# Where the powers of lam for waves 2 to 5 are computed, and which engine makes one of four turn copies

## The chip, the cores and the metric

The kernel runs on one core of a Trainium2 chip. The core has a matrix engine (TensorE, in the profile PE, with its weight loads as PEld), three engines for elementwise work (VectorE or DVE, ScalarE or ACT, GpSimd or POOL), and SyncE (SP), which here only issues transfers between the chip's main memory and the on-chip memory. ACT and POOL can issue transfers too. Each engine runs its own instructions in their order; engines wait for one another through semaphores. Matmul results land in a small accumulator memory (PSUM), everything else that is on the chip is in SBUF. The metric is device time in microseconds, as the median of several runs.

## The reference

Two stages. The first is a linear attention with a decay per head, over 4 batches, 8 heads, 768 positions and head size 64, worked in blocks of 64 positions:

```python
rel = pos[:, None] - pos[None, :]
Dmask = np.where(rel >= 0, lam[:, None, None] ** rel[None, :, :], 0.0)
lam_pow = lam[:, None, None] ** (pos[None, :, None] + 1)
for b in range(nb):
    intra = np.einsum('bhic,bhjc->bhij', qb, kb) * Dmask[None]
    intra = np.einsum('bhij,bhjd->bhid', intra, vb)
    inter = np.einsum('bhid,bhde->bhie', qb * lam_pow[None], kv_state)
    out[:, :, sl] = intra + inter
    kb_dec = kb * rev_pow[None]
    kv_state = lam_block[None, :, None, None] * kv_state + np.einsum('bhsd,bhse->bhde', kb_dec, vb)
```

`lam` has one value for each head, between 0.97 and 0.99. The second stage is an MLP on the 3072 rows of 512 that come out: `h = x @ w_in` (512 to 2048), `g = h * sigmoid(1.702 h)`, `g @ w_out` (2048 to 512).

## The kernel before

The work is cut into six waves of 512 rows. Wave 0 takes the first 256 positions of batches 0 and 1, wave 1 those of batches 2 and 3, and waves 2 to 5 take 128 further positions of all four batches each. In a wave the attention of its positions is computed in transposed form (`xT`), and the MLP runs on that. The list `main` (line 543 on) holds the MLP's matmul groups of all waves in order; the list `side` holds the attention of the next wave with a position in `main` at which each part is issued. So each engine's order is fixed when the kernel is built, and PE is meant to find MLP matmuls between the attention's short ones.

The kernel applies the decay by scaling k and q with powers of lam before the scores are taken. Waves 0 and 1 (`ND = 2`) use `kd_pow` and `qd_pow`; their casts are line 198. Waves 2 to 5 use four other tables:

- `k_pow` and `q_pow` (128 x 2 x 8: position x copy x head): lam to the power 127 - s and s + 1. Read by the casts of line 205.
- `inv_pow` (128 x 8): lam to the power -128. Read with the 0/1 mask by line 335.
- `blk_pow` (128 x 4): lam to the power 128 for the heads of each half. Read by the state update, line 355.

All tables are made at the start. `lam` (8 values) is loaded by a transfer on ACT's queue, spread over 128 partitions by a matmul with ones (`lam_p`, line 147), ACT takes the logarithm (`ln_lam`, line 149), and then each table is one or two ACT instructions, exp(scale * ln_lam), with the exponents of each position in small tables made by POOL's iota (`i_k`, `i_q`, lines 127 to 130). In the order of the code: kd_pow and qd_pow (line 152), then, as the first lines of the hand-written schedule, k_pow and q_pow (455), inv_pow (456), blk_pow (458). Line 460 is a GELU on one column, which makes ACT load the table set of the GELU before it is needed.

After that comes the hand-written start of wave 0. A "turn" is a transposition on PE into PSUM (`turn_pe`, line 228; its PE instructions are line 234) and a copy from there to SBUF by the engine that is passed as `copy` (ACT's copies bear line 217, DVE's line 214). For batch 0 k is cast and turned in two groups, and then q in two groups; all four copies are ACT's. `fill` issues matmuls on zeros, whose result nobody reads. `d_scores` makes scores on PE (255) and masks on DVE (259); `d_one`, `d_state`, `d_inter` and `d_out` make the block's state and output on PE (271, 290, 308). Batch 1 of the wave follows, its k cast by POOL, its q by DVE, with the copies of the second groups by DVE.

Transfers: SP issues the loads of k, q and v of wave 0 at once, batch 0 first. POOL waits for v's first element (`gate_pool`, line 447) and issues the loads of w_in (line 177) and, after batch 1's v cast, the rest of w_in and w_out (181). The last POOL instruction of this stretch is the affine_select that makes `mask` (502). SP's loads of wave 1 stand behind a small transfer that reads w_out's second part (`gate_sync`, line 450). POOL is used again for wave 1's v cast (line 211) and for one of its k casts.

Of the kernel before, what the change touches and what calls it, by code (L numbers as in the profile page):

```python
# [24 lines left out]
def kernel(  # L25
# [13 lines left out]
    nc = tc.nc  # L39
    f32 = mybir.dt.float32  # L40
    bf16 = mybir.dt.bfloat16
    B, H, S, D = q.shape
    P = 128
# [10 lines left out]
    EXP = mybir.ActivationFunctionType.Exp  # L54
    LN = mybir.ActivationFunctionType.Ln
    COPY = mybir.ActivationFunctionType.Copy
    GELU = mybir.ActivationFunctionType.Gelu_apprx_sigmoid
    MUL = mybir.AluOpType.mult
    ADD = mybir.AluOpType.add

    NW = S // P

    const = ctx.enter_context(tc.tile_pool(name="const", bufs=1))
# [4 lines left out]
    op = ctx.enter_context(tc.tile_pool(name="op", bufs=4))  # L68
# [39 lines left out]
    def iota(x, pattern, base, cm):  # L108
        nc.gpsimd.iota(x, pattern=pattern, base=base, channel_multiplier=cm, allow_small_or_imprecise_dtypes=True)

    A, Z = slice(0, 64), slice(64, P)
# [15 lines left out]
    i_k = const.tile([P, 1], f32)  # L127
    iota(i_k, [[0, 1]], P - 1, -1)
    i_q = const.tile([P, 1], f32)
    iota(i_q, [[0, 1]], 1, 1)  # L130
    mask = const.tile([P, 1, P], bf16)
    nc.gpsimd.memset(mask, 1.0)

# [2 lines left out]
    def acc(name, dt=f32, shape=None, tag="a"):  # L136
        return ps.tile(shape or [P, 4, P], dt, tag=tag, bufs={"a": 5, "mm": 3}[tag], name=name)

    def fill(n, new=None):
        if new:  # L140
            fill_ps[0] = acc("ps_fill", shape=[P, W], tag=new)
        for _ in range(n):
            nc.tensor.matmul(fill_ps[0], zero[:, 0:P], zero, start=True, stop=True)  # L143

    fill(4, "mm")
    lam_p = ps.tile([P, H], f32, tag="a", bufs=5, name="lam_p")
    nc.tensor.matmul(lam_p, ones, lam_r, start=True, stop=True)
    ln_lam = const.tile([P, H], f32)
    nc.scalar.activation(ln_lam, lam_p, LN)

    def mk_pow(x, scale):
        nc.scalar.activation(x, ln_lam, EXP, scale=scale)

    kd_pow = const.tile([P, H, 2], f32)
    qd_pow = const.tile([P, H, 2], f32)
# [3 lines left out]
    k_pow = const.tile([P, 2, H], f32)  # L159
    q_pow = const.tile([P, 2, H], f32)  # L160
    inv_pow = const.tile([P, H], f32)
    blk_pow = const.tile([P, NP], f32)
    warm = const.tile([P, 1], f32)
# [16 lines left out]
    def load_w_out(j):  # L180
        nc.gpsimd.dma_start(
            out=w_out_sb[j], in_=moe_w_out.rearrange("(fc fi) d -> fi fc d", fi=P)[:, j * CW : (j + 1) * CW, :])
# [6 lines left out]
    def do_cast(w, c, nm, eng, g=None):  # L189
        if g in (None, 0):  # L190
            cast[w, c, nm] = work.tile([P, 2, HD], bf16, tag=f"{nm}s{c}", name=f"{nm}s")
        f, x = loaded[w, c, nm], cast[w, c, nm]
        if w < ND:
            pw = {"k": kd_pow, "q": qd_pow}[nm]
            for R in (0, 1) if g is None else (g,):
                for j in range(2):
                    h = slice(4 * R + 2 * j, 4 * R + 2 * j + 2)
                    eng.tensor_tensor(x.rearrange("p a (r i j d) -> p r j i a d", i=2, j=2, d=D)[:, R, j],  # L198
                                      f[:, h].rearrange("p i (a d) -> p i a d", a=2),
                                      pw[:, h].unsqueeze(3).to_broadcast([P, 2, 2, D]), op=MUL)  # L200
        else:
            pw = {"k": k_pow, "q": q_pow}[nm]
            n = 2 * H // 4
            for j in range(2):
                eng.tensor_tensor(x.rearrange("p b (r i j d) -> p j (b r) i d", i=2, j=2, d=D)[:, j],  # L205
                                  f.rearrange("p h (a d) -> p (h a) d", a=2).rearrange("p (n j i) d -> p j n i d", j=2, i=2)[:, j],
                                  pw.rearrange("p b (r j i) -> p j (b r) i", i=2, j=2)[:, j].unsqueeze(3).to_broadcast([P, n, 2, D]),
                                  op=MUL)
# [19 lines left out]
    def turn_pe(w, c, nm, copy=act_copy, g=None):  # L228
        x = cast[w, c, nm]
        rr = list(range(NP)) if g is None else [2 * g, 2 * g + 1]  # L230
        t = acc("ps_t", bf16, [P, len(rr), 2, P])
        for i, r in enumerate(rr):
            for a in range(2):
                nc.tensor.transpose(t[:, i, a, :], x[:, a, r * P : (r + 1) * P], ident)  # L234
        if g in (None, 0):
            trans[w, c, nm] = work.tile([P, 2 * NP, P], bf16, tag=f"{nm}T{c}", name=f"{nm}T")
        copy(trans[w, c, nm][:, 2 * rr[0] : 2 * rr[0] + 2 * len(rr)], t.rearrange("p r a s -> p (r a) s"))
# [106 lines left out]
    def n_state(w, R):  # L344
# [8 lines left out]
        for i in range(2):  # L353
            p = 2 * R + i
            nc.vector.scalar_tensor_tensor(new[:, :, p, :], old[:, :, p, :], blk_pow[:, p : p + 1], ps_kv[:, i],  # L355
                                           op0=MUL, op1=ADD)

# [93 lines left out]
        nc.sync.dma_start(out=behind, in_=x)  # L451

    with tc.manual_schedule():
        for x, i in ((k_pow, i_k), (q_pow, i_q)):
            nc.scalar.activation(x, ln_lam.unsqueeze(1).to_broadcast([P, 2, H]), EXP, scale=i)
        mk_pow(inv_pow, -1.0 * P)
        for j, rows in enumerate((A, Z)):
            nc.scalar.activation(blk_pow[rows].rearrange("p (r i) -> p r i", i=2),
                                 ln_lam[rows].rearrange("p (r j i) -> p r j i", i=2, j=2)[:, :, j, :], EXP, scale=1.0 * P)
        nc.scalar.activation(warm, q_pow[:, 0, 0:1], GELU)  # L460
        fill(5)
        for g in range(2):
            do_cast(0, 0, "k", nc.vector, g)
# [1 line left out]
            fill(2)  # L465
        for g in range(2):
            do_cast(0, 0, "q", nc.vector, g)
            turn_pe(0, 0, "q", act_copy, g)
            fill(2 - 2 * g)
        gate_pool(loaded[0, 0, "v"][0:1, 0, 0:1])  # L470
        load_w_in(0)
# [27 lines left out]
            load_w_in(j)  # L499
        for j in range(NCH):  # L500
            load_w_out(j)
        nc.gpsimd.affine_select(mask, mask, pattern=[[0, 1], [1, P]], channel_multiplier=-1, base=0,
                                compare_op=mybir.AluOpType.is_ge, fill=0.0)
        gate_sync(w_out_sb[1][0:1, 0, 0:2])
# [15 lines left out]
        def end(w, c):  # L520
# [11 lines left out]
            if w:  # L532
                nc.vector.tensor_tensor(kv_sb[0][:, 2 * w + c], kept[w, c], t, op=ADD)
            else:
# [9 lines left out]
        for w in range(NW):  # L544
# [3 lines left out]
            x = w + 1  # L548
# [57 lines left out]
```

## Time and profile before

| | |
|---|---|
| median of 8 runs | 208.19 us (207.49 to 209.06) |
| the profiled execution's own time | 208.26 us |
| its span | 206.6 us |
| PE busy | 198.6 us (96%) |
| DVE, ACT, POOL busy | 89.2, 86.0, 16.1 us |
| ACT's activations for k_pow, q_pow, inv_pow, blk_pow | 4.89 to 5.78 us from the span's start |
| table load of line 460 | from 5.80 us, 1.28 us long |
| first MLP matmul group of the stretch that then runs without a gap | 18.45 us |
| casts of wave 1's k on DVE | from 38.04 us |
| first use of k_pow, inv_pow, blk_pow | 53.4, 66.0, 76.6 us |

Line numbers are those of the kernel before. In lines of a timeline the first number is the start in us from the span's start, the second the length in us; then come engine, line, operation, what is written and read, how many instructions are taken together, and in brackets how long the engine sat idle before them and what ended that. In the chain of what ended last, listed in order of time, the two numbers are start and length as well. An engine name with a q behind it (SPq, POOLq) is its issuing side. A line of a helper is used by many parts of the kernel, so tile names say more than lines.

### The profile page before, as it was taken

What the parts mean: (1) busy time and instruction counts of PE and PEld (TensorE: products, weight loads), DVE (VectorE), ACT (ScalarE), POOL (GpSimd) and SP (SyncE); (2) the same over time, 40 slices, a digit from 0 to 9 for tenths busy, and PEclk for the clock granted to TensorE, in tenths of its full rate; (3) what the DMA queues carried; (4) which work ended last, traced back from release to release, by engine and by line L of the source; (5) the groups of instructions that cost most, each with busy time, mean ns of one, the idle gap of its engine ahead of it and who ended that gap; (6) DMA issues with size and microseconds to landing.
All of it is one profiled execution on the core that took longest, in us unless ns stands there. A gap on an engine that the chain in (4) does not pass through costs nothing.

```text
span 206.6 us, 4269 instructions
## 1 busy us (share of the span) xinstructions
PE 198.6 (96%) x1806; PEld 104.9 (51%) x1830; DVE 89.2 (43%) x158; ACT 86.0 (42%) x158; POOL 16.1 (8%) x37
## 2 busy tenths in 40 slices
PE   7989999999999999999999999999999999999994
PEld 2567444467864464444464444464444454444453
DVE  1685000686952842931743931743841731100121
ACT  4956662157665030565030566021566021565000
POOL 4369000060000000000000000000000000000000
PEclk9999999999999999999999999999999999999999
DMA  5999999999997999879961389971360111100112
GB/s 155 317 234 179 182 204 236 316 321 232 242 220 185 224 245 261 193 180 253 234 195 51 107 183 257 220 205 52 102 155 0 40 64 51 51 0 0 54 51 102
DMA packets 87640, 33.82 MB, mean 164 GB/s; under 512 B 67398, under 2 KB 84678, under 8 KB 87622
## 3 DMA queue, kind: packets, MB, share of 16 engines
q1 hardware_dynamic: 82868, 29.37, 56.3%
q0 software_dynamic: 4752, 4.19, 13.2%
q8 instruction: 14, 0.23, 0.4%
q14 instruction: 4, 0.03, 0.1%
q10 hardware_dynamic: 2, 0.00, 0.0%
HBM read 27.26 MB, written 6.29 MB: 162 GB/s over the span
## 4 chain that ended last, share of the span: by engine, by line
PE 90%; DVE 4%; ACT 3%; issue 1%; ACTq 0%; DVEq 0%
PE ps_out L413 39%; PE ps_h L389 35%; PE ps_h L401 5%; DVE sm L259 2%; PE ps_s L327 2%; PE ps_o L377 2%; PE ps_t L234 1%; PE ps_o L364 1%; DVE o_sb L417 1%; PE ps_s L255 1%; PE ps_fill L143 1%; PE ps_o L308 1%; PE ps_kv L351 1%; ACT L460 1%; PE ps_kv L271 1%
## 5 line engine op out<-in xcount | busy, mean ns | idle before, releaser
L413 PE MATMUL ps_out<-w_out,g_sb 128*128 128x512 bf16 (+2 forms) x400 | 83.8, 362 | 1.1 <-issue 0.6
L389 PE MATMUL ps_h<-xT,w_in 128*128 128x512 bf16 x330 | 73.2, 379 | 0.3
L391 ACT ACTIVATE g_sb<-ps_h 128x512 bf16<-128x512 f32 x84 | 50.2, 597 | 45.1 <-PE ps_h L389 45.1
L413 PEld LDWEIGHTS <-g_sb 128*128 128x128 bf16 x416 | 38.2, 98 | 41.0
L389 PEld LDWEIGHTS <-w_in 128*128 128x128 bf16 x336 | 32.9, 98 | 39.2
L417 DVE COPY o_sb<-ps_out 128x512 f32<-128x512 f32 (+2 forms) x26 | 16.9, 650 | 52.4 <-PE ps_out L413 52.3
L335 DVE SCALAR_TENSOR_TENSOR sm<-ps_s,inv_pow,mask 128x512 bf16<-128x512 f32 x32 | 21.8, 743 | 28.5 <-PE ps_s L327 22.3
L381 ACT CAST xT<-ps_o 128x512 bf16<-128x512 f32 x16 | 8.2, 599 | 37.8 <-PE ps_o L377 37.8
L198 DVE TENSOR_TENSOR ks<-kf,kd_pow 128x256 bf16<-128x256 f32 x8 | 2.9, 421 | 22.0 <-DMA kf<-in_k_dram 18.7
L401 PE MATMUL ps_h<-xT,w_in 128*128 128x256 bf16 x96 | 11.4, 273 | 0.0
L259 DVE TENSOR_TENSOR sm<-ps_s,mask_d 128x512 bf16<-128x512 f32 x16 | 9.9, 683 | 1.9 <-PE ps_s L255 1.8
L205 DVE TENSOR_TENSOR qs<-qf,q_pow 128x512 bf16<-128x512 f32 x16 | 10.3, 684 | 0.0
L205 DVE TENSOR_TENSOR ks<-kf,k_pow 128x512 bf16<-128x512 f32 x16 | 10.3, 683 | 0.0
L401 PEld LDWEIGHTS <-w_in 128*128 128x128 bf16 x96 | 9.0, 98 | 1.7 <-DVE xT L214 0.2
L403 ACT ACTIVATE g_sb<-ps_h 128x512 bf16<-128x512 f32 x12 | 7.2, 597 | 4.4 <-PE ps_h L401 4.3
L143 PE MATMUL ps_fill<-zero 128*128 128x512 bf16 x18 | 6.9, 510 | 1.4 <-DVE zero L113 1.4
L355 DVE SCALAR_TENSOR_TENSOR kv<-kv,blk_pow,ps_kv 128x256 bf16<-128x256 bf16 x12 | 5.0, 477 | 6.0 <-PE ps_kv L351 6.0
L217 ACT COPY kT<-ps_t 128x512 bf16<-128x512 bf16 (+1 forms) x5 | 3.7, 752 | 7.7 <-PE ps_t L234 7.7
L198 DVE TENSOR_TENSOR qs<-qf,qd_pow 128x256 bf16<-128x256 f32 x16 | 6.0, 428 | 1.1 <-DMA qf<-in_q_dram 1.0
L327 PEld LDWEIGHTS <-kT 64*128 64x128 bf16 x128 | 3.6, 94 | 3.4 <-issue 3.4
L214 DVE CAST v_sb<-vf 128x1024 bf16<-128x1024 f32 x8 | 5.1, 685 | 0.0
L327 PE MATMUL ps_s<-qT,kT 64*128 64x128 bf16 x128 | 5.0, 217 | 0.0
(66 smaller groups left out, 88.7 us busy)
## 6 DMA issues: line engine op xcount, KB each, us to landing
vf<-in_v_dram SPq DMA_DIRECT2D x11, 512.0 KB, 6.5
kf<-in_k_dram SPq DMA_DIRECT2D x10, 512.0 KB, 5.7
qf<-in_q_dram SPq DMA_DIRECT2D x10, 512.0 KB, 6.4
out_dram<-o_sb SPq DMA_DIRECT2D x15, 256.0 KB, 2.0
out_dram<-o_sb SPq DMA_DIRECT2D x17, 128.0 KB, 2.4
w_out<-in_moe_w_out_dram POOLq DMA_DIRECT2D x4, 512.0 KB, 13.8
w_in<-in_moe_w_in_dram POOLq DMA_DIRECT2D x3, 512.0 KB, 6.8
kf<-in_k_dram SPq DMA_DIRECT2D x4, 256.0 KB, 3.1
```

Source lines behind the costliest of these rows:

```text
L143: nc.tensor.matmul(fill_ps[0], zero[:, 0:P], zero, start=True, stop=True)
L198: eng.tensor_tensor(x.rearrange("p a (r i j d) -> p r j i a d", i=2, j=2, d=D)[:, R, j], f[:, h].rearrange("p i (a d) -> p i a d", a=2), p ...
L205: eng.tensor_tensor(x.rearrange("p b (r i j d) -> p j (b r) i d", i=2, j=2, d=D)[:, j], f.rearrange("p h (a d) -> p (h a) d", a=2).rearran ...
L259: nc.vector.tensor_tensor(sm.rearrange("p i a s -> p i (a s)"), s2[h].rearrange("p (i a) s -> p i (a s)", i=2), mask_d.rearrange("p o a b ...
L327: nc.tensor.matmul(s2[h][:, b, :], kT[hs, (b % 2) * NP + p, :], qT[hs, (b % 2) * NP + p, :], start=True, stop=True)
L335: nc.vector.scalar_tensor_tensor(sm, s, inv_pow[:, n : n + 1], mask.to_broadcast([P, B, P]), op0=MUL, op1=MUL)
L381: nc.scalar.copy(xT[w][:, p, :], ps_o.rearrange("p b s -> p (b s)"))
L389: nc.tensor.matmul(h, w_in_sb[j][:, kc, i * P : (i + 1) * P], xT[w][:, kc, :], start=(kc == 0), stop=(kc == KC - 1))
L391: nc.scalar.activation(g_of[w][:, fc, :], h, GELU)
L401: nc.tensor.matmul(h[:, u, :], w_in_sb[j][:, kc, i * P : (i + 1) * P], xT[w][:, kc, cols], start=(kc == 0), stop=(kc == KC - 1))
L413: nc.tensor.matmul(ps_out, g_of[w][:, fc, g * P : (g + 1) * P], w_out_sb[j][:, fc % CW, c0:c1], start=(fc == 0), stop=(fc == FFC - 1))
L417: nc.vector.tensor_copy(o, ps_out)
```

## The change

The four tables of waves 2 to 5 are no longer made by ACT. DVE copies the spread lam from PSUM to SBUF (`lam_s`), and POOL, behind its last issue of w_out and ahead of the affine_select for `mask`, computes lam to the power of the exponents directly with `pow` of two tensors: one half of k_pow, one half of q_pow, and inv_pow (exponents in the new constant `i_c`). It copies the halves to the second halves, and makes blk_pow as the product of k_pow and q_pow, whose exponents add up to 128. The GELU on one column now follows qd_pow and reads it. And of the four turn copies of batch 0 in wave 0, that of q's second group is made by DVE.

```diff
+    POW = mybir.AluOpType.pow
...
+    i_c = const.tile([P, 1], f32)
+    nc.gpsimd.memset(i_c, -1.0 * P)
...
+    lam_s = const.tile([P, H], f32)
+    nc.vector.tensor_copy(lam_s, lam_p)
     ln_lam = const.tile([P, H], f32)
     nc.scalar.activation(ln_lam, lam_p, LN)
...
-        for x, i in ((k_pow, i_k), (q_pow, i_q)):
-            nc.scalar.activation(x, ln_lam.unsqueeze(1).to_broadcast([P, 2, H]), EXP, scale=i)
-        mk_pow(inv_pow, -1.0 * P)
-        for j, rows in enumerate((A, Z)):
-            nc.scalar.activation(blk_pow[rows].rearrange("p (r i) -> p r i", i=2),
-                                 ln_lam[rows].rearrange("p (r j i) -> p r j i", i=2, j=2)[:, :, j, :], EXP, scale=1.0 * P)
-        nc.scalar.activation(warm, q_pow[:, 0, 0:1], GELU)
+        nc.scalar.activation(warm, qd_pow[:, 0, 0:1], GELU)
...
-            turn_pe(0, 0, "q", act_copy, g)
+            turn_pe(0, 0, "q", (act_copy, dve_copy)[g], g)
...
+        for x, i in ((k_pow[:, 0, :], i_k), (q_pow[:, 0, :], i_q), (inv_pow, i_c)):
+            nc.gpsimd.tensor_tensor(x, lam_s, i.to_broadcast([P, H]), op=POW)
+        for x in (k_pow, q_pow):
+            nc.gpsimd.tensor_copy(x[:, 1, :], x[:, 0, :])
+        for j, rows in enumerate((A, Z)):
+            kp, qp = [x[rows, 0, :].rearrange("p (r j i) -> p r j i", i=2, j=2)[:, :, j, :] for x in (k_pow, q_pow)]
+            nc.gpsimd.tensor_tensor(blk_pow[rows].rearrange("p (r i) -> p r i", i=2), kp, qp, op=MUL)
         nc.gpsimd.affine_select(mask, mask, pattern=[[0, 1], [1, P]], channel_multiplier=-1, base=0,
                                 compare_op=mybir.AluOpType.is_ge, fill=0.0)
```

## The prediction

> **What bounds the kernel now.** I read the page first (busy shares, then the chain that ended last), then the chain of the first 19 us in order of time, then the timelines of ScalarE (ACT), VectorE (DVE), GpSimd (POOL) and TensorE (PE) there and around 38 us, since that is as far as the change's effects can run before something else sets the clock.
>
> ```profile
> PE 198.6 (96%) x1806; PEld 104.9 (51%) x1830; DVE 89.2 (43%) x158; ACT 86.0 (42%) x158; POOL 16.1 (8%) x37
> PE 90%; DVE 4%; ACT 3%; issue 1%; ACTq 0%; DVEq 0%
> ```
>
> PE holds 90% of the chain, and the change doesn't touch PE's work. What can be won lies in the 3% of ACT and what follows it. The start of the chain:
>
> ```profile
> 4.11 0.49 ACT kd_pow L152 x2
> 4.60 0.38 ACT qd_pow L152 x2
> 4.98 0.20 ACT k_pow L455
> 5.80 1.28 ACT L460
> 7.30 0.96 ACT kT L217 x2
> 8.26 0.50 ACT qT L217
> 8.80 0.47 PE ps_s L255 x16
> 9.33 2.49 DVE sm L259 x4
> ```
>
> From 4.1 to 8.8 us ACT is the chain: powers, the table load of the GELU warm-up (L460), three turn copies; then PE's first scores and DVE's four masks. Here the change removes work. But the chain follows what ended last; it doesn't say how far behind the second-latest condition is. The two places downstream where the work joins a transfer do:
>
> ```profile
> 6.59 1.51 DVE L198 TENSOR_TENSOR qs<-qf,qd_pow 128x256 bf16<-128x256 f32 x4 [0.52 <-DMA qf<-in_q_dram]
> 11.73 0.90 DVE L198 TENSOR_TENSOR qs<-qf,qd_pow 128x256 bf16<-128x256 f32 x2
> 13.14 0.76 DVE L198 TENSOR_TENSOR qs<-qf,qd_pow 128x256 bf16<-128x256 f32 x2 [0.51 <-DMA qf<-in_q_dram]
> 14.39 0.42 DVE L214 COPY qT<-ps_t 128x512 bf16<-128x512 bf16 x1 [0.16 <-PE ps_t L234]
> 14.96 1.29 DVE L259 TENSOR_TENSOR sm<-ps_s,mask_d 128x512 bf16<-128x512 f32 x2
> ...
> 38.04 0.76 DVE L198 TENSOR_TENSOR ks<-kf,kd_pow 128x256 bf16<-128x256 f32 x2 [18.72 <-DMA kf<-in_k_dram]
> 39.05 0.42 DVE L198 TENSOR_TENSOR ks<-kf,kd_pow 128x256 bf16<-128x256 f32 x1
> 39.52 0.23 PEld L234 LDWEIGHTS <-ks 128*128 128x128 bf16 x4
> ```
>
> At 13.14 DVE has waited 0.51 us for the second half of batch 1's q; at 38.04 it has waited 18.72 us for wave 1's k. The last cast of that k ends at 39.05 + 0.42 = 39.47, and the weight load of PE's fifth turn begins at 39.52. PE's first four turns start from 39.26 on, some 0.06 us apart, so its own queue is ready for the fifth at about 39.5: there PE arrives just as the data do.
>
> **The change, part by part.**
>
> *ACT's preamble.* Removed: k_pow, q_pow, inv_pow and two blk_pow activations. The qd_pow pieces end at 4.98, the table load starts at 5.80: 0.82 us less ahead of the load. The load then runs 4.98 to 6.26 and the warm activation (0.20) to 6.47. It reads qd_pow, which is ready. The first k turn leaves PE at 6.46, so the copies go from being held by ACT to being held by PE: kT group 0 6.50 to 7.09 (0.59 each), group 1 after its turn at 7.19, 7.23 to 7.82; qT group 0 after its turn at 7.85, 7.89 to 8.48.
>
> *One turn copy moves to DVE.* q's group 1 is turned by PE from 8.15 to 8.55, because its cast is held by qf's landing at 6.59 and DVE's four casts to 8.10. DVE has nothing else until 9.33 (it idles 1.23 us there), so the copy takes 8.59 to 9.01 (0.42, the row at 14.39). Queued behind it are the four masks. ACT loses one step of about 0.5 us and gets to v's casts at 8.5 instead of 9.11 (v has landed by 8.11, when POOL's gate on it ran).
>
> *First scores.* They need kT and qT group 0 (8.48 + 0.04) and PE's queue free of the last turn (8.55): 8.60 instead of 8.80. The first mask came 0.53 after the scores: 9.13, later than the copy's end at 9.01, so the moved copy doesn't hold it. **Gain here 0.20 us, not 0.82**: the rest goes into waiting for q's transfer and PE's turns. The masks end at 11.62 instead of 11.82.
>
> *Where that 0.20 goes.* DVE's next casts start 0.20 earlier and the one after them waits for qf, which still lands at 13.1: its issue is on SP's queue at 7.27 with nothing of the change before it. The wait grows from 0.51 to 0.71. From there the order is cast, turn at 13.96, DVE copy to 14.81, masks at 14.96, unchanged. The chain names ACT's kv copy (14.20) as what released the scores at 14.50; if that is right they can move to 14.4, and the masks to about 14.81, where DVE's copy ends: at most 0.15 us. If the filler matmul in front of them holds them (its record isn't in the trace), nothing moves. I take 0.05.
>
> *What is left reaches PE at 39.4.* PE is busy without a gap from 18.5 to 39.4 and would come up to 0.15 us earlier to wave 1's k, whose arrival is set by SP's issue at 32.17, which stands behind a gate on w_out's landing (31.35), which stands behind POOL's issues from 16.23 on, which stand behind v's landing (15.68). None of these waits for work of the change. The fifth turn follows the cast by 0.05 us already, so **0.00 to about 0.04 us is left for the span**.
>
> *POOL.* One more memset of 128x1 in the preamble (about 0.1 us, ahead of 4.73 us of idle), and seven instructions after the last w_out issue: three pow, two copies, two products. They are queued past no DMA issue that was there before; the mask's affine_select stands behind them, and its first reader is L335 at 66.0.
>
> ```profile
> 19.91 0.79 POOL L181 DMA_DIRECT2D w_out<-in_moe_w_out_dram  x1
> 20.65 0.35 POOL L502 TENSOR_SCALAR_AFFINE_SELECT mask<-mask 128x128 bf16<-128x128 bf16 x1
> 41.13 1.17 POOL L211 CAST v_sb<-vf 128x512 bf16<-128x512 f32 x2 [20.13 <-DMA vf<-in_v_dram]
> ```
>
> The cover is POOL's 20.13 us of idle. No pow is in the trace. Below: as cheap as a plain POOL instruction, 0.1 to 0.2 us each (iota 128x1 0.14). Above: no row bounds it. POOL's product L198 takes 0.605 us for 256 columns, 2.4 ns a column; a pow of eight columns at 100 times that is 1.9 us. I take 1 us for each pow and 0.15 for the other four, 3.6 us, all hidden: it ends at 24.3. The first reader of k_pow is at 53.4, of blk_pow at 76.6. **The cover breaks** when the seven take more than 20.1 us plus the 0.6 between the v casts' end (42.30) and PE's state matmuls (42.96): 20.7 us, or 6.7 us for each pow, 0.84 us a column. Past that point each us is a us on the end, as PE's in-order queue stands at those matmuls.
>
> [...] The trace shows that POOL and DVE disturb each other: DVE's cast at 11.73, beside a product on POOL, took 0.569 us against a median of 0.418. [...] By the row a collision costs 0.15 us for an instruction[...]. It costs nothing while the pows end before 38.04: DVE runs nothing between 19.3 (the end of its cast at 18.63) and 38.04. [...]
>
> *DVE.* The added copy lam_s (128x8 from PSUM) can start with ln_lam at 3.83 and takes some 0.1 to 0.2 us in a 3.31 us wait for kd_pow that ends at 4.63: nothing. Without that cover it would delay the k casts by its length.
>
> **Sum.** The profiled execution took 208.26 us for a span of 206.6, so 1.66 lies around it. Span 206.6 - 0.02 = 206.58, and 208.24 by that execution; the median of the runs is 0.07 below the profiled one, so 208.17. I write 208.15.
>
> **Rivals.**
> *The waits for transfers don't hold.* If in most executions the transfers come earlier, ACT's saving passes. The 0.20 passes to 207.99, still no measurable change. The whole 0.82 gives 207.37. For it: the chain names ACT all the way from 4.11 to 8.76. Against: DVE waits for qf at 6.59 and at 13.14, and for kf at 38.04, all in one trace.
> *Pow is dear.* At 8 us each, 24 + 0.6 = 24.6 us, 3.9 more than the cover: 212.1, slower. It decides from 6.7 us for each pow; contention with the casts at 38.04 begins a little earlier, from 5.6 us. For it: no row bounds a pow from above. Against: eight columns are very few.
> *The turn copy on DVE holds the masks.* If PE's last turn or the copy runs late, masks start late. Cover: 0.12 us at the first mask, then the 0.71 us of waiting at 13.14; a copy that is 0.83 us late costs nothing, and one that is 1.5 us late costs 0.7: 208.9. Against: DVE copies of this shape took 0.42 twice.
> *The change doesn't do what it says.* If ACT's table load stays at 5.8, because it waits for something other than the five activations, the time is 208.19.
>
> **How the numbers follow.** Absorbed, as forecast: 0.58. Doesn't do what it says: 0.03. The partial gain of 0.1 to 0.3 passes: 0.08. A gain near 0.8 passes: 0.11. Pow past its cover or in DVE's way: 0.12. Late masks or another small loss: 0.08. A measurement of this kernel tells about 0.3% (0.62 us) from no change. The cases give faster 0.12, same 0.68, slower 0.20. The first three alone would be 207.8 to 208.5. The range reaches down to the full gain, 207.4, and up through the late masks and the collision with the casts, 209.2; it leaves out the dear pow and the ends of the gain.
>
> **What would show it.** Table load at 5.0 and copies on ACT at 6.5, else the preamble step is wrong. First scores at 8.6, DVE's copy of qT before the first mask at 9.1. DVE's wait for qf at 13.1 at 0.7 us, masks of batch 1 at 14.8 to 15.0. First MLP matmuls at 18.4 to 18.5, wave 1's k casts at 38.0 and its turns at 39.5 as before. POOL's seven instructions between 20.65 and about 24, and the v cast at 41.1. The prediction falls if the pows reach 38 us, or if wave 1's casts move: then something of the change reaches the transfers, which I hold to be independent of it.

## The result, and the profile after

The changed kernel takes 210.26 us (median of 11 runs, 209.49 to 212.0) against 208.16 us before (32 runs): a ratio of 1.0106, with a 95% interval of 1.008 to 1.0132. It is slower by about 2 us where no change was forecast, and outside the range. The profiled execution has a span of 207.9 us (209.82 us with what lies around it), 1.3 more than before. The ratios here and below, and the median of 11, leave disturbed executions out (one of 12 here, 212.8 us); the medians of the experiments do not.

A small part of the loss, some 0.2 us, lies outside the span; the section on why the prediction was wrong has the numbers.

The page of the changed kernel, busy shares and the chain that ended last:

```profile
PE 198.9 (96%) x1806; PEld 104.9 (50%) x1830; DVE 90.2 (43%) x160; ACT 84.7 (41%) x152; POOL 21.7 (10%) x45
PE 70%; DMA 15%; SPq 7%; ACT 2%; issue 1%; DVE 1%; POOL 1%
```

PE does the same work, but it holds 70% of the chain instead of 90%. Transfers, which had no share of it before, hold 15%, and SP's issuing 7%. This share says where to look, and not how much was lost: a version below that is as fast as the kernel before (ratio 0.9991) has 13% and 4% there.

The start, as ACT and DVE ran it in the changed kernel (start, length, instruction, idle time before it):

```profile
4.03 0.18 ACT L154 ACTIVATE ln_lam<-lam_p 128x8 f32<-128x8 f32 x1 [1.41 <-DVE lam_s L152]
5.20 1.28 ACT L459 ACT_TABLE_LOAD   x1
6.61 1.05 ACT L222 COPY kT<-ps_t 128x512 bf16<-128x512 bf16 x2
...
8.57 0.42 DVE L219 COPY qT<-ps_t 128x512 bf16<-128x512 bf16 x1 [0.49 <-PE ps_t L239]
8.99 2.48 DVE L264 TENSOR_TENSOR sm<-ps_s,mask_d 128x512 bf16<-128x512 f32 x4
11.86 1.91 DVE L203 TENSOR_TENSOR qs<-qf,qd_pow 128x256 bf16<-128x256 f32 x4 [0.39 <-DMA qf<-in_q_dram]
14.83 2.48 DVE L264 TENSOR_TENSOR sm<-ps_s,mask_d 128x512 bf16<-128x512 f32 x4
```

This part went as forecast in outline: the first masks start 0.34 us earlier, and batch 1's masks start at 14.83 instead of 14.96. In between it did not: the wait for q's transfer is 0.39 us at 11.86, not 0.71 at 13.14, and the first of the four casts there takes 0.90 us beside a product on POOL. POOL's seven instructions end long before wave 1's v cast, which still waits for its transfer:

```profile
19.59 1.73 POOL L502 TENSOR_TENSOR k_pow<-lam_s,i_k 128x8 f32<-128x8 f32 x1
21.25 1.67 POOL L502 TENSOR_TENSOR q_pow<-lam_s,i_q 128x8 f32<-128x8 f32 x1
22.86 1.66 POOL L502 TENSOR_TENSOR inv_pow<-lam_s,i_c 128x8 f32<-128x8 f32 x1
...
25.27 0.29 POOL L508 TENSOR_SCALAR_AFFINE_SELECT mask<-mask 128x128 bf16<-128x128 bf16 x1
41.64 1.17 POOL L216 CAST v_sb<-vf 128x512 bf16<-128x512 f32 x2 [16.07 <-DMA vf<-in_v_dram]
```

So the time was lost elsewhere. The table of transfer queues (packets, MB, and the time of its packets as a share of 16 engines' span), before:

```profile
DMA packets 87640, 33.82 MB, mean 164 GB/s; under 512 B 67398, under 2 KB 84678, under 8 KB 87622
q1 hardware_dynamic: 82868, 29.37, 56.3%
q0 software_dynamic: 4752, 4.19, 13.2%
```

and after:

```profile
q1 hardware_dynamic: 82868, 29.37, 67.4%
q0 software_dynamic: 4752, 4.19, 12.9%
```

The median load of q of 512 KB lands later, 7.6 us behind its issue instead of 6.4 (before, then after):

```profile
qf<-in_q_dram SPq DMA_DIRECT2D x10, 512.0 KB, 6.4
qf<-in_q_dram SPq DMA_DIRECT2D x10, 512.0 KB, 7.6
```

The queue that SP fills moves the same 82868 packets and the same 29.37 MB, and takes a fifth longer for them: 0.563 x 16 x 206.6 us / 82868 = 22.5 ns for a packet before, 0.674 x 16 x 207.9 / 82868 = 27.1 ns after. POOL's queue is as before. No instruction of the change issues a transfer. Where the slower transfers reach PE, in the changed kernel's timeline:

```profile
15.86 1.05 PE L406 MATMUL ps_h<-xT,w_in 128*128 128x256 bf16 x8 [0.70 <-DMA w_in<-in_moe_w_in_dram]
38.10 1.43 DVE L203 TENSOR_TENSOR ks<-kf,kd_pow 128x256 bf16<-128x256 f32 x4 [18.52 <-DMA kf<-in_k_dram]
47.09 1.14 ACT L222 CAST v_sb<-vf 128x512 bf16<-128x512 f32 x2 [2.53 <-DMA vf<-in_v_dram]
66.97 0.23 PE L332 MATMUL ps_s<-qT,kT 64*128 64x128 bf16 x2 [0.58 <-DMA qT<-qs]
```

The k casts of wave 1 (38.10) are where they were. The loads behind them on SP's queue slip one after the other: wave 1's last v casts start at 47.09 instead of 45.59, and the last transposing transfer for wave 2 is issued at 62.60 instead of 60.23 (before, then after; the third line is wave 2's first scores before, without a wait):

```profile
60.23 1.25 SPq L241 DMA_TRANSPOSE qT<-qs  x1
62.60 1.28 SPq L246 DMA_TRANSPOSE qT<-qs  x1
65.53 0.62 PE L327 MATMUL ps_s<-qT,kT 64*128 64x128 bf16 x16
```

By PE's timeline and the chain the loss is 0.26 us at the MLP's stretch (18.71 against 18.45), 0.59 at wave 1's second scores (51.14 against 50.55) and 1.33 behind wave 2's first scores (67.48 against 66.15). From there it stays, up to the end of the span (1.3).

### The profile page after: what moved, and what is told of

Its sections match the earlier page's. It is cut to its first block, busy times and chain, and to the rows that moved or that the text cites. A ratio compares the mean times of both kernels' runs of the same rounds, so it can differ in the third digit from the quotient of the medians.

```text
span 207.9 us, 4274 instructions
## 1 busy us (share of the span) xinstructions
PE 198.9 (96%) x1806; PEld 104.9 (50%) x1830; DVE 90.2 (43%) x160; ACT 84.7 (41%) x152; POOL 21.7 (10%) x45
## 2 busy tenths in 40 slices
DMA packets 87640, 33.82 MB, mean 163 GB/s; under 512 B 67398, under 2 KB 84678, under 8 KB 87622
## 3 DMA queue, kind: packets, MB, share of 16 engines
q1 hardware_dynamic: 82868, 29.37, 67.4%
## 4 chain that ended last, share of the span: by engine, by line
PE 70%; DMA 15%; SPq 7%; ACT 2%; issue 1%; DVE 1%; POOL 1%
PE ps_out L418 32%; PE ps_h L394 28%; SPq L82 7%; DMA vf<-in_v_dram 7%; DMA w_out<-in_moe_w_out_dram 7%; PE ps_h L406 3%; PE ps_s L332 2%; DMA qT<-qs 2%; PE ps_o L382 2%; PE ps_o L369 1%; DVE o_sb L422 1%; PE ps_kv L356 1%; ACT v_sb L222 1%; ACT qT L222 0%; ACT kT L222 0%
## 5 line engine op out<-in xcount | busy, mean ns | idle before, releaser
L210 DVE TENSOR_TENSOR qs<-qf,q_pow 128x512 bf16<-128x512 f32 x16 | 10.3, 683 | 0.0
L210 DVE TENSOR_TENSOR ks<-kf,k_pow 128x512 bf16<-128x512 f32 x16 | 10.3, 683 | 0.0
## 6 DMA issues: line engine op xcount, KB each, us to landing
w_out<-in_moe_w_out_dram POOLq DMA_DIRECT2D x4, 512.0 KB, 14.6
```

## The experiments

The two new constants take room. In the built programs each tile of `const` begins at a multiple of 32 bytes of its partition, so `i_c` (4 bytes) and `lam_s` (32 bytes) take 64 bytes together, and every tile allocated behind them lies 64 bytes further on. There the tiles that k, q and v are loaded into (`kf`, `qf`, `vf`) all begin at multiples of 256 bytes before (64768 for the first) and 64 bytes behind one after (64832). That gives the theory: **the new addresses slow SP's transfers**. Its rivals: the moved instructions change the order in which transfers run and collide; or transfers simply differ from one execution to the next.

**Addresses undone, instructions kept.**

```diff
-    i_k = const.tile([P, 1], f32)
+    i_all = const.tile([P, 8], f32)
+    i_k, i_q, i_c = [i_all[:, j : j + 1] for j in range(3)]
+    lam_s = const.tile([P, H], f32)
...
-    i_q = const.tile([P, 1], f32)
...
-    i_c = const.tile([P, 1], f32)
...
-    lam_s = const.tile([P, H], f32)
```

> The changed kernel with its two new constants packed into room that was free, so that every tile from the mask on lies at the address that it has in the kernel before; instructions as in the changed kernel. If the addresses are the cause (all tiles behind the new constants moved by 64 bytes): 208.1 to 208.3 us, as first forecast, and the SP queue's share of the 16 transfer engines back from 67% to about 56%. If the moved instructions are the cause: 210.0 to 210.5 us and 66 to 68%.

Measured: ratio 1.0023 (0.9997 to 1.0049), median 208.91 us.

**Addresses moved, instructions of before.**

```diff
+    pad_a = const.tile([P, 1], f32)
+    nc.gpsimd.memset(pad_a, 1.0)
     mask = const.tile([P, 1, P], bf16)
     nc.gpsimd.memset(mask, 1.0)
+    pad_b = const.tile([P, 8], f32)
+    nc.vector.memset(pad_b, 1.0)
```

> The kernel before with two unused constants of 4 and 32 bytes, which move all later tiles by 64 bytes, as the change does; no other instruction changed but a memset on GpSimd and one on VectorE for them. If the addresses are the cause: 210.0 to 210.5 us, and a share of about 67% on SP's queue. If the moved instructions are: 208.1 to 208.3 us and about 56%.

Measured: ratio 1.0102 (1.0064 to 1.0139), median 210.40 us. The loss of the change is there with nothing of its work. The queue's row of the run with the addresses undone:

```profile
q1 hardware_dynamic: 82868, 29.37, 56.2%
```

and of this one:

```profile
q1 hardware_dynamic: 82868, 29.37, 65.9%
```

**Moved by 256 bytes** (`pad_b` of 56 columns instead of 8).

> The same as the run before with a larger second constant, so that all later tiles move by 256 bytes. If only the position within 256 bytes counts: 208.1 to 208.3 us and about 56%. If any move counts, or if the two memsets do: about 210.3 us.

Measured: ratio 0.9992 (0.9969 to 1.0015), share 56.4%. So neither the memsets nor a move as such costs anything.

**The kernel before, a second profile.**

> The kernel before, unchanged, for a second profile. If the share of SP's queue is a trait of the kernel: 55 to 58% of 16 engines. If it is one of the execution: it can be anywhere between 56% and 68%, and then the comparison of the two profiles says nothing.

Measured: share 57.0%, one time of 208.99 us. So the share belongs to the kernel, not to the execution, and every profile below agrees; chance is out.

**Which tiles.** First the weights and v_sb moved, the loads back at a multiple of 256 (the changed kernel with unused bytes at the end of its constants):

```diff
     seen = const.tile([P, 1], f32)
+    pad_c = const.tile([P, 48], f32)
+    nc.vector.memset(pad_c, 1.0)
```

> The changed kernel with 192 unused bytes behind its last constant: w_in, w_out, v_sb stay moved by 64 bytes, the tiles of k, q and v, and all behind them, move on to a multiple of 256 bytes again. If it is the position of those tiles that counts: 208.2 to 208.9 us, a share of 56 to 57% on SP's queue. If it is the weights' position: 210 to 210.5 us and a longer way to landing for w_in and w_out (8.3 and 14.6 us, as in the changed kernel). If both: between them.

Measured: ratio 1.0011 (0.9982 to 1.004), share 56.3%. Landing of w_in and w_out was even later than in the changed kernel (9.2 and 15.5 us against 8.3 and 14.6), without a loss of time. The two profiles of the kernel before differ as much (6.8 and 13.8, 9.1 and 15.5 us), so their landing says little here.

Then only the loads moved (16 columns of padding at the end of the constants, and 96 bytes for each buffer in the loads' own pool, which put all tiles behind it back):

```diff
+    pad_c = const.tile([P, 16], f32)
+    nc.vector.memset(pad_c, 1.0)
...
+    for _ in range(2):
+        pad_d = ld.tile([P, 24], f32, tag="pad", name="pad_d")
+        nc.vector.memset(pad_d, 1.0)
```

> The kernel before with only the tiles that k, q and v are loaded into moved by 64 bytes; the weights are unmoved and all tiles behind the loads at a multiple of 256 as before. If the loads' position is the cause: 209.6 to 210.4 us, and most of the 10 points of share (62 to 66%). If it is the tiles of the transposing transfers or of the stores: 208.1 to 208.5 us and 56 to 58%.

Measured: ratio 1.0117 (1.007 to 1.0164), share 64.8%. The tiles of k, q and v are enough for the whole loss. The transposing transfers of k land after 2.8 us here as before (3.4 in the changed kernel), those of q after 3.2 (2.7 before, 3.3 in the changed kernel); whether the moved tiles that these read and write account for the rest of the share is open. For time they don't, as far as the interval tells.

**How far from a multiple of 256.** Moved by 128 (`pad_b` of 24 columns), and by 32 (no `pad_a`, `pad_b` of 8):

> The kernel before with all later tiles moved by 128 bytes. [...] as with 64: about 210.4 us and a share of 64 to 67%. If multiples of 128 are enough: 208.1 to 208.4 us and 56 to 58%.

> The kernel before with all tiles behind the mask moved by 32 bytes. [...] a share of 64 to 67% on SP's queue, as with 64. If a finer alignment matters too: above 68%. The one time tells little beside the share.

Measured: by 128, ratio 1.0106 (1.0079 to 1.0133), share 65.4%; by 32, share 67.6%, one time of 210.87 us. No distance that was tried is free, and none stands out; for 32 bytes only the share and one time say so. PE's wait for a transposed q at wave 2's first scores stands in the profiles of the four kernels whose loads lie 64 or 128 bytes off a multiple of 256 (0.58 to 1.06 us); with the loads at a multiple, one profile of nine has it, at 0.18.

**Weights at a multiple of 256 too** (24 columns of padding behind `warm`, 40 behind `seen`, in the kernel before).

> The kernel before with the weights (w_in, w_out, which begin 160 bytes behind a multiple of 256) moved to a multiple of 256 as well, and the rest moved by 256. If the position counts for the weights' transfers too: they land earlier than after 6.8 and 13.8 us, and the time is 207.0 to 207.9 us. If it counts only for the loads on SP's queue: 208.1 to 208.3 us.

Measured: ratio 0.9985 (0.9956 to 1.0014), share of POOL's queue 13.2% as before, landing 8.5 and 14.7 us. No gain can be told.

**What the moved work is worth.** The changed kernel with the old addresses and the copy of lam behind the logarithm:

```diff
-    nc.vector.tensor_copy(lam_s, lam_p)
     ln_lam = const.tile([P, H], f32)
     nc.scalar.activation(ln_lam, lam_p, LN)
+    nc.vector.tensor_copy(lam_s, lam_p)
```

> The changed kernel with the addresses of the kernel before, and with the copy of lam from PSUM placed behind the logarithm, which in the changed kernel waited for it (4.03 instead of 3.83 us). If my account of the moved instructions holds (absorbed by q's and k's transfers): 208.0 to 208.4 us, ratio to the kernel before within 0.3% of 1. If they cost something of their own that the addresses hid: above 208.7 us. If they win the 0.8 us of the preamble: 207.4 us.

Measured: ratio 0.9991 (0.9959 to 1.0024), median 208.06 us. The logarithm is back at 3.84 us. Its profile shows where the early start ends: in waits for transfers, at the first MLP group and at wave 1's k, behind which PE itself now waits for DVE's casts.

```profile
15.49 1.05 PE L405 MATMUL ps_h<-xT,w_in 128*128 128x256 bf16 x8 [0.51 <-DMA w_in<-in_moe_w_in_dram]
38.38 1.43 DVE L202 TENSOR_TENSOR ks<-kf,kd_pow 128x256 bf16<-128x256 f32 x4 [19.19 <-DMA kf<-in_k_dram]
39.87 0.40 PE L238 MATMUL ps_t<-ident,ks 128*128 128x128 bf16 x4 [0.27 <-DVE ks L202]
```

With the weights' and loads' addresses at multiples of 256 as well:

> The changed kernel with lam's copy behind the logarithm and with the weights and the loads at multiples of 256 bytes. If what was gained at the start is absorbed by the transfers: 208.0 to 208.4 us, a ratio within 0.3% of 1. If the aligned weights land earlier and let the gain through: 207.3 to 207.8 us.

Measured: ratio 0.9998 (0.9973 to 1.0024), median 208.17 us. No version of the change can be told to beat the kernel before.

**The cover of the pows.** Each pow issued six times over, same values:

```diff
+            for _ in range(6):
                 nc.gpsimd.tensor_tensor(x, lam_s, i.to_broadcast([P, H]), op=POW)
```

> The changed kernel with the addresses of the kernel before, lam's copy behind the logarithm, and each pow done six times over (eighteen pows instead of three; same values). At 1.65 us each GpSimd is busy from 20.3 to about 51 us, 10 us past the start of wave 1's v cast at 41.1. If that cover is the limit, as forecast, the span grows by 9 to 10 us (about 216 us). If something else covers more: less.

Measured, in one execution: span 218.2 us (219.94 us), 11.3 more than in the profile without the repeats.

From its timeline, its table of waits (us in total, times, longest), and its table of stretches (the third number from the end is the granted clock):

```profile
51.81 1.16 POOL L215 CAST v_sb<-vf 128x512 bf16<-128x512 f32 x2
```

```profile
PE ps_kv L275 <- POOL v_sb L215: 10.1, 2, 9.8
```

```profile
52.90:58.00 5.10, 4.97 (x67) 3.02 (x67) 3.82 (x8) 1.84 (x5) 2.37 (x5) 0.62 0.86 196
```

The v cast comes 10.3 us later than the 41.47 of the run without repeats, and PE waits 10.1 us for it at the state matmuls: the place and size that the cover had. That leaves 1.2 us. In the 5.1 us behind the wait PE's granted clock is 0.62 (1.00 in the run without repeats from 43 to 48 us); by my estimate that costs at most 5.1 x 0.38 = 1.9 us, so it can account for the 1.2, which is not shown further.

## Why the prediction was wrong

**The step that failed** is "None of these waits for work of the change", and its conclusion that the transfers are independent of it. As to waits it is true: no transfer is seen to wait for work of the change. But the change reached the transfers by where it put its data. The sum counted the new memset at 0.1 us and the copy of lam at nothing, and did not count the 64 bytes that their two tiles take. Moving the bytes alone gives 1.0102, the instructions alone 0.9991 to 1.0023, and both 1.0106: as far as these intervals can tell, the bytes are the whole loss. The sign that I had named for this, moved casts of wave 1's k, did not show it (38.10 against 38.04): I followed the transfers to 39.5 us only, and most of the loss came behind that.

What makes these packets take longer was not shown. k, q and v come in rows of 512 bytes for waves 0 and 1 and of 256 bytes for the others (67398 of 87640 packets are under 512 bytes, those of other transfers among them). Tiles moved by 32, 64 and 128 bytes all cost, tiles moved by 256 nothing, and the share of SP's queue does not rise with the distance (67.6, 65.9 and 65.4%). Over the whole queue a packet takes a fifth longer, 27.1 ns instead of 22.5. The profiles give that time by queue alone, so they do not say which rows pay, nor where on the way from main memory to the tile.

**What lies around the span** was a smaller term that the sum carried over unchanged, as 1.66 us. In all 86 executions of the changed kernel and its four versions without repeats it is 1.82 to 1.94 us, 1.88 on average, with the loads' tiles moved or not. In all 175 with the instructions of before it is 1.65 to 1.78 us, 1.71 on average, with the tiles moved or not. So some 0.18 us, 0.1% of the time, goes with the moved work and not with the addresses. The one execution with the repeated pows has 1.74, and the cause is open.

**ACT's preamble** held in kind. The saving was 0.60 instead of 0.82 (table load at 5.20, not 4.98), because ln_lam waited for DVE's copy, which I had let run beside it: 4.03 instead of 3.83. That 0.20 also delays kd_pow and the k casts (4.83 instead of 4.63). The order is the program's and not the chip's: both only read lam_p, and in the built program the one that stands second waits for the first one's semaphore. With the copy behind the logarithm it is DVE that waits (4.04, released by ln_lam).

**First scores and the turn copy** held: the copy ran at 8.57 to 8.99 (forecast 8.59 to 9.01), with the masks right behind it at 8.99 instead of 9.13.

**Where the 0.20 goes** held in its end only: at the old addresses nothing is left of it. On the way there the term for q was wrong. The wait of 0.51 us at 13.14 was one execution's: the second profile of the kernel before doesn't have it, nor do the runs with the work moved and the addresses of before. With the addresses undone DVE casts q without a wait from 11.28, and batch 1's masks start at 13.90, 1.06 us earlier than in the profile before. What takes that is a place that I had not named, w_in's landing at the first MLP group (1.44 us of waiting there, 0.51 in the run with lam's copy behind the logarithm), and behind it wave 1's k, which I had named:

```profile
11.28 1.56 DVE L202 TENSOR_TENSOR qs<-qf,qd_pow 128x256 bf16<-128x256 f32 x4
15.67 1.05 PE L405 MATMUL ps_h<-xT,w_in 128*128 128x256 bf16 x8 [1.44 <-DMA w_in<-in_moe_w_in_dram]
```

So the forecast that nothing is left came out with a wrong place in it, and in that was lucky. Four versions of the moved work lie between 0.9991 and 1.0023, all with 1 inside the interval; whether the order of the copy of lam is worth the 0.2% between them is open.

**POOL** held. A pow was mis-sized: 1.6 to 1.7 us from start to start instead of 1, the seven together 5.7 us (19.59 to 25.27) instead of 3.6, and still 16 us short of the end of the cover. The first pow took 1.73 us, the other two 1.67 and 1.66. The repeats put the break where the sum had it.

**The rivals**: none was the cause. They asked when a transfer starts and who waits for it; none had a transfer that itself takes longer. The price of a collision of POOL and DVE, 0.15 us for a cast by the one row that I had, was too low: 0.48 in the changed kernel (0.90 against a median of 0.42), 0.39 in the second profile of the kernel before. No cast met a pow, so the pows cost nothing in this way.

## What to carry to other kernels

When a change adds or drops an on-chip tile, list the addresses of the tiles that transfers fill, before and after; a constant of 4 bytes can move them all (here by 32). Put such tiles at multiples of 256 bytes on purpose (here 22.5 ns a packet on SP's queue there, and 27.1 at 64 bytes off), or give small constants the free columns of a tile that exists. And before a time is put down to the instructions of a change, run its data layout alone with the old instructions: one run settled here what the trace alone could not.

## What was not expected of the hardware

- SP's transfers took 27.1 ns a packet instead of 22.5 when the tiles they fill begin 64 bytes off a multiple of 256. The five kernels whose k, q and v tiles lie off a multiple had shares of 64.8 to 67.6% on that queue; those at a multiple had 56.2 to 57.0% (52.9% in the run of 218 us, over its longer span).
- For POOL's transfers of the weights, no effect of the position could be told (13.2% at 160 bytes behind a multiple of 256 and at 0).
- A DVE cast of q (`qs<-qf,qd_pow`) that met a product on POOL (`ks<-kf,kd_pow`) ended 0.3 us behind the end of that product (12.30 and 12.01 in the kernel before, 12.76 and 12.47 in the changed one), so that it took 0.57 us in the one and 0.90 in the other.
- PE's filler matmuls reach their later pace (0.59 us for two, from 7.03 on in the profile before, against 1.06 at 4.98) at a moment that differs between executions. The two at 6.2 us took 0.71 and 0.85 us together in two profiles of the kernel before, 0.59 with the addresses undone and 1.06 with lam's copy behind the logarithm, all in profiles with a mean granted clock of 1.00; in the last two the first scores started at 8.35 and 9.20. The MLP's stretch began at 18.50 and 18.32 all the same, behind the wait for w_in.
